# Joining the two halves of each weighted-sum run in a fused LSH attention and mixture-of-experts kernel

## The chip, the core and the metric

The kernel runs on one core of one Trainium2 chip. The metric is the device time of one execution in microseconds (us). Five engines work side by side, each through its own instructions in order: TensorE (PE; its weight loads are listed as PEld), VectorE (DVE), ScalarE (ACT), GpSimd (POOL) and SyncE (SP), which issues most transfers. They meet at semaphores only.

## The reference

```python
# q, k, v: [4, 8, 768, 64]; proj: [64, 6]
q_bucket = bits of (q @ proj > 0);  k_bucket = bits of (k @ proj > 0)
scores = where(q_bucket == k_bucket, q @ k.T / 8, -1e9)
attn = exp(scores - rowmax);  attn /= rowsum + 1e-9
x = attn @ v                      # 3072 tokens of 512
e = argmax(x @ w_gate);  g = softmax(x @ w_gate)[e] * sigmoid(x @ w_output_gate)[e]
out = g * (relu(x @ w1[e]) @ w2[e])      # one expert of 8 for each token
```

## The kernel before, in words

There are 32 heads, taken as 16 pairs. A pair has 12 steps, 192 steps in all; one step is one block of 128 queries of one head against its 768 keys. The order of each engine's work is written out by hand: the program order is the order on each engine.

What one step does, on four engines:

- `scores` (L534): four groups of matmuls (L546) make the 128x768 scores and the bucket penalty in PSUM tile `ps_s` (two buffers). VectorE caps them, copies them to `sc` and takes the row minimum `mn` (L550).
- `soft` (L553): ScalarE takes the exponential of `sc` and its row sum (L558).
- `normal` (L562): for two steps together, VectorE makes the reciprocal of the sums (L565, L566) and GpSimd scales `sc` (L568).
- `transposed` (L570), for the step LAG = 4 earlier: TensorE transposes the six 128x128 blocks of `sc` (L579) into two `ps_t` tiles (two buffers, three blocks each), and ScalarE copies each tile to `pts` (L580).

Six steps are a half pair: 384 queries of both heads. When its `pts` are complete, `weighted` (L582) multiplies them with `v`, chunk by chunk of 128 keys (L590): six chunks, two heads side by side, each head on 64 columns of the array, all added up in `ps_a` (one buffer). `RUN` = 3 puts chunks 0 to 2 at one step and chunks 3 to 5 three steps later. After the last chunk ScalarE copies `ps_a` to `ot` (L593).

The positions in a half pair are counted here from the step that holds chunk 0: position 0 is a step s with (s - 4) divisible by 6, the next ones are positions 1 to 5. The second group of chunks is at position 3.

Side work, hung on step numbers by `plan` (at the end of a step) or `plan_ahead` (before the normalising of a step):

- For the next pair: `project` (L405) on TensorE, 128x32 weights into `ps_m` (one buffer), `threshold` (L415) on VectorE, `split_hi` (L489) on GpSimd, four `split_lo` (L498) on VectorE, and `spread` (L506), transfers on SP that build the operands of the scores.
- `rows` (L595): VectorE transposes `ot` and SP writes it to `x_dram`.
- For each batch of four pairs the routing: `logits` (L618; 128x32 weights, copied to `lt` by ScalarE), `tokens` (L628), `best`, `choose`, `prefix`, `softmax_sum`, `gates`, `ranks`, `cols`, `hot`, `table`, `entries`. Most of it is small VectorE work; `logits`, `tokens`, `prefix` and `table` are TensorE's. `pick` (L769) chooses the first expert after the third batch.

The loop that runs a step (L873 to L895) decides where the exponentials stand: after the transposes of positions 2 and 5 (the steps ahead of a run), and behind the chunks at positions 0 and 3. So there are three exponentials around every group of three chunks.

After the last step the last half pair's chunks, its routing and the first expert's first layer are mixed by hand (L909 to L947): `fill` (L903) is one block of that layer, and the weights `w2` come in through the two `w_raw` buffers. Then eight experts follow.

## Time and profile before

| | |
|---|---|
| median of three runs | 781.82 us (781.23 to 781.83) |
| profiled execution | 783.98 us, of which span 782.2 us |
| TensorE / ScalarE / VectorE / GpSimd busy | 97% / 61% / 58% / 46% of the span |
| mean granted TensorE clock | 0.991 |

The span is the profile's own length of the execution. A busy TensorE is not a TensorE at its peak, since matmuls overlap and their ends are modelled; what a stretch costs is read from the distance between starts of the same instruction.

### The profile page before, as it was taken

What the parts mean: (1) busy time and instruction counts of PE and PEld (TensorE: products, weight loads), DVE (VectorE), ACT (ScalarE), POOL (GpSimd) and SP (SyncE); (2) the same over time, 40 slices, a digit from 0 to 9 for tenths busy, and PEclk for the clock granted to TensorE, in tenths of its full rate; (3) what the DMA queues carried; (4) which work ended last, traced back from release to release, by engine and by line L of the source; (5) the groups of instructions that cost most, each with busy time, mean ns of one, the idle gap of its engine ahead of it and who ended that gap; (6) DMA issues with size and microseconds to landing.
All of it is one profiled execution on the core that took longest, in us unless ns stands there. A gap on an engine that the chain in (4) does not pass through costs nothing. (4 is left out here: it accounts for less than half of the span.)

```text
span 782.2 us, 13687 instructions
## 1 busy us (share of the span) xinstructions
PE 761.1 (97%) x4706; PEld 604.8 (77%) x4706; DVE 451.6 (58%) x1003; ACT 478.9 (61%) x968; POOL 361.9 (46%) x415
## 2 busy tenths in 40 slices
PE   8999999999999999999999989799999999999996
PEld 6677776777766777766777668688999999989894
DVE  6666656666765776766677544146263636455540
ACT  6888888888878888788887731143252524343331
POOL 6564544454443445444455542632537363736301
PEclk9999999999999999999999999899999999999998
DMA  4544555565445556544554232353445444436411
GB/s 164 150 130 90 129 135 97 123 147 139 95 114 132 97 128 146 129 95 116 139 113 123 72 77 109 88 194 114 145 149 157 152 148 153 157 142 208 169 50 40
DMA packets 84799, 98.89 MB, mean 126 GB/s; under 512 B 57999, under 2 KB 59439, under 8 KB 84720
## 3 DMA queue, kind: packets, MB, share of 16 engines
q1 hardware_dynamic: 79376, 84.58, 41.2%
q0 software_dynamic: 5200, 13.31, 5.2%
q8 instruction: 40, 0.66, 0.3%
q14 instruction: 39, 0.32, 0.1%
q10 hardware_dynamic: 144, 0.02, 0.0%
HBM read 59.49 MB, written 13.11 MB: 93 GB/s over the span
## 5 line engine op out<-in xcount | busy, mean ns | idle before, releaser
L568 POOL TENSOR_SCALAR sc<-sc,rsum 128x768 f32<-128x768 f32 x192 | 172.6, 911 | 220.9 <-DVE rsum L566 126.1
L550 DVE TENSOR_SCALAR_CACHE_REDUCE sc<-ps_s 128x768 f32<-128x768 f32 x192 | 183.6, 957 | 124.2 <-PE ps_s L546 117.1
L580 ACT COPY pts<-ps_t 128x384 f32<-128x384 f32 x384 | 165.1, 483 | 67.8 <-PE ps_t L579 67.8
L558 ACT ACTIVATE sc<-sc,mn 128x768 f32<-128x768 f32 x192 | 178.2, 936 | 10.1 <-DVE sc L550 9.8
L579 PEld LDWEIGHTS ps_t<-ident,sc 128*128 128x128 f32 x1152 | 130.4, 140 | 49.3 <-issue 32.2
L579 PE MATMUL ps_t<-ident,sc 128*128 128x128 f32 x1152 | 161.6, 276 | 2.8 <-POOL sc L568 1.9
L590 PE MATMUL ps_a<-pts,vt 128*64 128x384 f32 x768 | 138.0, 494 | 0.4 <-ACT pts L580 0.4
L546 PE MATMUL ps_s<-xr,xl 128*128 128x384 f32 x384 | 114.9, 380 | 1.0 <-DVE sc L550 1.0
L546 PE MATMUL ps_s<-yr,yl 76*128 76x384 f32 x384 | 99.0, 338 | 0.2
L313 PE MATMUL ps_s<-xh,w1h 128*128 128x256 f32 (+7 forms) x288 | 97.2, 337 | 2.0 <-DVE mx L650 1.2
L590 PEld LDWEIGHTS ps_a<-pts,vt 128*64 128x64 f32 x768 | 49.4, 136 | 61.0 <-issue 54.4
L313 PE MATMUL ps_s<-xh,w1l 128*128 128x256 f32 (+7 forms) x288 | 95.2, 331 | 0.8 <-issue 0.8
L324 DVE SCALAR_TENSOR_TENSOR hl<-ps_s,hh 128x256 fp32r<-128x256 f32 (+8 forms) x40 | 34.0, 849 | 107.0 <-ACT hh L323 94.7
L313 PE MATMUL ps_s<-xlo,w1h 128*128 128x256 f32 (+7 forms) x288 | 95.4, 331 | 0.0
L287 POOL DMA_INDIRECT xq<-x_dram,idx x75 | 81.5, 1086 | 21.6 <-issue 20.5
L330 POOL DMA_INDIRECT out_dram<-yo,sid x29 | 32.3, 1113 | 126.9 <-ACT yo L329 65.3
L323 ACT ACTIVATE hh<-ps_s 128x256 fp32r<-128x256 f32 (+8 forms) x40 | 28.9, 725 | 91.1 <-PE ps_s L313 73.2
L546 PEld LDWEIGHTS ps_s<-xr,xl 128*128 128x128 f32 x384 | 58.0, 191 | 16.7 <-DVE sc L550 7.5
L546 PEld LDWEIGHTS ps_s<-yr,yl 76*128 76x128 f32 x384 | 69.9, 189 | 0.7 <-POOL yr L446 0.7
L313 PEld LDWEIGHTS ps_s<-xh,w1h 128*128 128x128 f32 x288 | 54.2, 188 | 4.6 <-issue 2.0
L313 PEld LDWEIGHTS ps_s<-xlo,w1h 128*128 128x128 f32 x288 | 54.1, 188 | 1.3 <-DVE xlo L270 0.2
L313 PEld LDWEIGHTS ps_s<-xh,w1l 128*128 128x128 f32 x288 | 54.1, 188 | 1.2
(204 smaller groups left out, 996.5 us busy)
## 6 DMA issues: line engine op xcount, KB each, us to landing
w_raw<-in_w_dram SPq DMA_DIRECT2D x36, 512.0 KB
qk<-in_qkT_dram SPq DMA_DIRECT2D x32, 384.0 KB
xh<-in_w_dram SPq DMA_DIRECT2D x14, 512.0 KB
xlo<-in_w_dram SPq DMA_DIRECT2D x14, 512.0 KB
vt<-in_v_dram SPq DMA_DIRECT2D x16, 384.0 KB
xr<-xl SPq DMA_DIRECT2D x30, 192.0 KB
yr<-xl SPq DMA_DIRECT2D x30, 192.0 KB
xr<-yl SPq DMA_DIRECT2D x30, 192.0 KB
```

Source lines behind the costliest of these rows:

```text
L287: nc.gpsimd.indirect_dma_start(out=xq[:, k * P:(k + 1) * P], out_offset=None, in_=x_dram.rearrange("n (a f) -> (n a) f", a=NB32), in_offse ...
L313: nc.tensor.matmul(ps, l, r, start=first and k == 0, stop=last and k == len(pairs) - 1)
L323: nc.scalar.activation(hh, ph, AF.Relu)
L324: return lambda: nc.vector.scalar_tensor_tensor(hl, ph, 0.0, f32(hh), ALU.max, ALU.subtract)
L330: nc.gpsimd.indirect_dma_start(out=out[:, :], out_offset=bass.IndirectOffsetOnAxis(ap=sid[0:n, r, a:a + 1], axis=0), in_=yo[0:n], in_offse ...
L546: nc.tensor.matmul(ss[:, n, 0:HS], l[0:k, qs], r[0:k, n * HS:(n + 1) * HS], start=first, stop=not first)
L550: nc.vector.tensor_scalar(sc, ss[:, :, 0:HS], MASKED, None, ALU.min, ALU.min, accum_out=mn)
L558: nc.scalar.activation(pr, pr, AF.Exp, bias=mn, scale=-1.0, accum_out=sums[s // GROUP][:, k:k + 1])
L568: nc.gpsimd.tensor_scalar(live[s0 + k], live[s0 + k], rs[:, k:k + 1], 0.0, ALU.mult, ALU.add)
L579: nc.tensor.transpose(tr[:, c], pr[:, (3 * h + c) * P:(3 * h + c + 1) * P], ident)
L580: nc.scalar.copy(pts[:, 3 * h:3 * h + 3, t * P:(t + 1) * P], tr)
L590: nc.tensor.matmul(st["av"][j * D:(j + 1) * D], st["v"][:, j, c], blocks[hb][j][:, c], start=(c == 0), stop=(c == NT - 1))
```

## The change

The six chunks of a half pair become one run, at position 0. Projections of the next pair, and the second logits of a batch, stand in the run behind the chunks. `threshold` follows behind the run. All four `split_lo` of a pair stand before or in the middle of the VectorE work ahead of the run, and so do `choose`, `ranks`, `cols`, `hot`, `softmax_sum`, `gates`, `entries`. The copies of `ot` and of the logits' `lt` go from ScalarE to VectorE. The exponentials move: one after position 1, one after position 3, three after position 5, one in the run.

```diff
                                      start=True, stop=True)
-                nc.scalar.copy(st["lt"][0:32 * n, cs], pm[0:32 * n])
...
+        def copies():
+            while summed_up:
+                summed_up.pop(0)(nc.vector.tensor_copy)
+
+        for g in range(NP):
+            for hf in range(2 if g + 1 < NP else 1):
+                for c in range(NT):
+                    plan_run(12 * g + 6 * hf + 6 + LAG, lambda hb=2 * g + hf, c=c: weighted(hb, c))
         for g in range(NP):
             s0 = 12 * (g - 1)
             if g >= 2:
                 plan(s0 - 9, lambda g=g: load(g))
-            if g >= 1:
-                hi, lo, sent = ((-1, 2), (4, 4, 4, 7), (4, 7)) if g > 1 else ((2, 4), (4, 5, 6, 7), (5, 7))
-                s0 += g == 1
-                plan(s0 if g > 1 else 3, lambda g=g: project(g))
-                plan(s0 + 1 if g > 1 else 3, lambda g=g: threshold(g))
+                plan_run(s0 + 4, lambda g=g: project(g))
+                plan_behind(s0 + 4, lambda g=g: threshold(g))
                 plan(s0 + 10, lambda g=g: load_v(g))
                 for j in range(2):
-                    plan(s0 + hi[j], lambda g=g, j=j: split_hi(g, j))
+                    plan(s0 + (-1, 2)[j], lambda g=g, j=j: split_hi(g, j))
                     for n in range(2):
-                        (plan_ahead if g > 1 else plan)(s0 + lo[2 * j + n], lambda g=g, j=j, n=n: split_lo(g, j, n))
-                    plan(s0 + sent[j], lambda g=g, j=j: spread(g, j))
-            for hf in range(2 if g + 1 < NP else 1):
-                for c in range(NT):
-                    products.setdefault(12 * g + 6 * hf + 6 + LAG + c // RUN * RUN, []).append(
-                        lambda hb=2 * g + hf, c=c: weighted(hb, c))
-                if g + 1 < NP:
-                    plan(12 * g + 25, lambda g=g, hf=hf: rows(g, hf))
+                        (plan_middle if j else plan_ahead)(s0 + 4, lambda g=g, j=j, n=n: split_lo(g, j, n))
+                    plan(s0 + (4, 5)[j], lambda g=g, j=j: spread(g, j))
+            elif g == 1:
+                plan(3, lambda: project(1))
+                plan(3, lambda: threshold(1))
+                plan(11, lambda: load_v(1))
+                for j in range(2):
+                    plan((3, 5)[j], lambda j=j: split_hi(1, j))
+                    for n in range(2):
+                        plan(5 + 2 * j + n, lambda j=j, n=n: split_lo(1, j, n))
+                    plan((6, 8)[j], lambda j=j: spread(1, j))
+            if g + 1 < NP:
+                for hf in range(2):
...
         for b in range(B - 1):
             r = routing(b)
-            ns = ((2, 4, 8, 9, 10, 13, 19, 25, 22, 22, 34, 34, 35, 35) if b == B - 2 else
-                  (2, 4, 8, 9, 10, 22, 22, 31, 34, 34, 46, 46, 47, 47))
-            for n, fn in zip(ns, (lambda r=r: r["logits"](0, H // 2), lambda r=r: r["tokens"](0, H // 2),
-                                  lambda r=r: r["logits"](1, H // 2), lambda r=r: r["tokens"](1, H // 2),
-                                  r["best"], r["choose"], r["softmax_sum"], r["gates"], r["prefix"], r["ranks"],
-                                  r["cols"], r["hot"], r["table"], r["entries"])):
-                (plan_ahead if n % 3 == 1 and n != 4 else plan)(12 * (H // 2) * (b + 1) + n, fn)
+            s0 = 12 * (H // 2) * (b + 1)
+            soon = b == B - 2
+            plan(s0 + 5, lambda r=r: r["logits"](0, H // 2), copies)
+            plan_run(s0 + 10, lambda r=r: r["logits"](1, H // 2))
+            for hf in range(2):
+                plan(s0 + 7 + 5 * hf, lambda r=r, hf=hf: r["tokens"](hf, H // 2))
+            plan(s0 + 13, r["best"])
+            plan_ahead(s0 + 16, r["choose"])
+            plan(s0 + 17, r["prefix"])
+            plan_middle(s0 + 22, r["softmax_sum"], r["gates"])
+            plan_ahead(s0 + 22, r["ranks"])
+            plan_ahead(s0 + (28 if soon else 34), r["cols"])
+            plan_middle(s0 + (28 if soon else 34), r["hot"])
+            plan(s0 + (30 if soon else 36), r["table"])
+            plan_ahead(s0 + (34 if soon else 40), r["entries"])
 
         r = routing(B - 1)
         s0 = 12 * (NP - 1)
         lp = H // 2 - 1
-        for d, fn in ((4, lambda: r["logits"](0, lp)), (6, lambda: r["tokens"](0, lp)), (8, lambda: r["logits"](1, lp)),
-                      (9, lambda: r["tokens"](1, lp))):
-            plan(s0 + d, fn)
+        for hf in range(2):
+            plan_run(s0 + 4 + 6 * hf, lambda hf=hf: r["logits"](hf, lp))
...
         plan_ahead(late, pick)
-        plan(late + 14, early_gather)
+        plan(late + 15, early_gather)
         for cc in range(NCC):
             plan(late + (1 + cc if cc < 2 else 18), lambda cc=cc: early_load(cc))
-            plan(late + (9, 12, 22, 23)[cc], lambda cc=cc: early_hi(cc))
-            plan_ahead(late + 18 + 6 * (cc // 2), lambda cc=cc: early_lo(cc))
+            plan(late + (9, 10, 22, 23)[cc], lambda cc=cc: early_hi(cc))
+            (plan_middle if cc % 2 else plan_ahead)(late + 18 + 6 * (cc // 2), lambda cc=cc: early_lo(cc))
         for a in range(EARLY):
-            plan(late + 21 + 3 * a, lambda a=a: early_turn(a))
...
-            def softs():
-                while late_soft:
-                    s = late_soft.pop(0)
+            def softs(n):
+                for s in late_soft[:n]:
                     live[s] = soft(s, *live[s])
                     if s % GROUP == GROUP - 1:
                         summed.append(s + 1 - GROUP)
+                del late_soft[:n]
+
+            def normals(n):
+                for s in summed[:n]:
+                    normal(s)
...
-                for fn in ahead.get(s, ()):
-                    fn()
-                while summed:
-                    normal(summed.pop(0))
                 if s in products:
+                    normals(1)
+                    for fn in ahead.get(s, ()):
+                        fn()
+                    normals(GROUP)
+                    for fn in middle.get(s, ()):
+                        fn()
                     for fn in products[s]:
                         fn()
-                    softs()
-                    while summed_up:
-                        summed_up.pop(0)(nc.scalar.copy)
+                    softs(1)
+                    copies()
+                    for fn in behind.get(s, ()):
+                        fn()
+                else:
+                    normals(GROUP)
                 if 0 <= s - LAG < NSTEP:
                     transposed(s - LAG, live.pop(s - LAG))
-                if s < 6 + LAG or s + 1 in products or s >= NSTEP - 1:
-                    softs()
+                since = (s - LAG) % 6
+                if s < 6 + LAG or s >= NSTEP - 1:
+                    softs(GROUP)
+                elif since:
+                    softs((0, 1, 0, 1, 0, 3)[since])
                 for fn in at.get(s, ()):
```

`plan_middle`, `plan_run` and `plan_behind` fill lists like `plan_ahead` does; `products` is the list of a run. `mn` gets 8 buffers instead of 4.

## Rows read from the trace of the kernel before

**Rows 1.** Windows by stage: microseconds from the span's start, and for PE, PEld, DVE, ACT and POOL the busy time with the count of instructions, then the granted TensorE clock as a share, the DMA share and GB/s. The row is the stretch from the first run to the run of step 190.

```profile
27.00:438.00 411.00, 409.76 (x2777) 291.69 (x2777) 275.53 (x745) 336.27 (x766) 194.66 (x246) 1.00 0.51 119
```

**Rows 2.** Timeline of TensorE's matmuls, positions 1 to 4 of a half pair: start, length, engine, line, what, count.

```profile
206.05 0.60 PE L546 MATMUL ps_s<-xr,xl 128*128 128x384 f32 x2
...
206.84 0.82 PE L579 MATMUL ps_t<-ident,sc 128*128 128x128 f32 x6
207.41 0.60 PE L546 MATMUL ps_s<-xr,xl 128*128 128x384 f32 x2
...
208.28 2.16 PE L590 MATMUL ps_a<-pts,vt 128*64 128x384 f32 x12
210.37 0.87 PE L579 MATMUL ps_t<-ident,sc 128*128 128x128 f32 x6
211.00 0.60 PE L546 MATMUL ps_s<-xr,xl 128*128 128x384 f32 x2
...
211.87 0.85 PE L579 MATMUL ps_t<-ident,sc 128*128 128x128 f32 x6
212.47 0.42 PE L546 MATMUL ps_s<-xr,xl 128*128 128x384 f32 x1
```

**Rows 3.** Timeline of TensorE's weight loads in that run of three chunks; a chunk takes two such rows.

```profile
208.66 0.14 PEld L590 LDWEIGHTS ps_a<-pts,vt 128*64 128x64 f32 x2 [0.18 <-issue]
...
209.63 0.14 PEld L590 LDWEIGHTS ps_a<-pts,vt 128*64 128x64 f32 x2 [0.18 <-issue]
```

**Rows 4.** Timeline of TensorE: starts of runs. The first and the last are those of steps 10 and 190, 60 runs apart; the three between follow one another.

```profile
27.09 2.16 PE L590 MATMUL ps_a<-pts,vt 128*64 128x384 f32 x12 [0.41 <-ACT pts L580]
...
67.03 2.16 PE L590 MATMUL ps_a<-pts,vt 128*64 128x384 f32 x12
73.34 2.16 PE L590 MATMUL ps_a<-pts,vt 128*64 128x384 f32 x12
...
438.22 2.16 PE L590 MATMUL ps_a<-pts,vt 128*64 128x384 f32 x12
```

**Rows 5.** Timeline of TensorE: a projection between the transposes and the next scores.

```profile
220.91 0.82 PE L579 MATMUL ps_t<-ident,sc 128*128 128x128 f32 x6
221.66 0.85 PE L411 MATMUL ps_m<-qk,pjc 128*32 128x384 f32 x8
222.44 0.44 PE L546 MATMUL ps_s<-xr,xl 128*128 128x384 f32 x1
```

**Rows 6.** Timeline of ScalarE. The first two rows are of the first steps, where an exponential stands between the copies of two steps; the others are around the run of rows 2.

```profile
20.19 0.96 ACT L558 ACTIVATE sc<-sc,mn 128x768 f32<-128x768 f32 x1
...
21.12 0.87 ACT L580 COPY pts<-ps_t 128x384 f32<-128x384 f32 x2
...
207.37 0.86 ACT L580 COPY pts<-ps_t 128x384 f32<-128x384 f32 x2 [0.50 <-PE ps_t L579]
208.11 0.94 ACT L558 ACTIVATE sc<-sc,mn 128x768 f32<-128x768 f32 x1
...
210.88 0.46 ACT L593 COPY ot<-ps_a 128x384 f32<-128x384 f32 x1
211.24 0.87 ACT L580 COPY pts<-ps_t 128x384 f32<-128x384 f32 x2
```

**Rows 7.** Timeline of TensorE in the first steps: the transposes that waited for the copy of the second of rows 6.

```profile
21.75 0.85 PE L579 MATMUL ps_t<-ident,sc 128*128 128x128 f32 x6
```

**Rows 8.** Timeline of VectorE: the read of the scores of the step whose matmuls start at 207.41.

```profile
208.39 0.96 DVE L550 TENSOR_SCALAR_CACHE_REDUCE sc<-ps_s 128x768 f32<-128x768 f32 x1 [0.39 <-PE ps_s L546]
```

**Rows 9.** Groups of instructions by line, engine and operation: shapes, count, busy us, mean ns of one, idle time before them and what ended it. VectorE's work that moves.

```profile
L503 DVE SCALAR_TENSOR_TENSOR yl<-qk,pj,xl 128x384 fp32r<-128x384 f32 x60 | 38.9, 685 | 0.0
L602 DVE STREAM_TRANSPOSE xb<-ot 128x384 f32<-128x384 f32 x32 | 16.7, 557 | 0.9 <-ACT ot L593 0.7
L418 DVE TENSOR_SCALAR bt<-ps_m,pj 128x384 fp32r<-128x384 f32 x15 | 9.6, 641 | 0.0
L593 DVE COPY ot<-ps_a 128x384 f32<-128x384 f32 x1 | 0.6, 558 | 1.9 <-PE ps_a L590 1.9
```

**Rows 10.** Timeline of VectorE: first instruction of `ranks`, and the sum's instruction behind `ranks` and `pick` (twelve instructions between them); first instruction of `cols`, and the sum's instruction behind `cols` and `hot`.

```profile
382.37 0.20 DVE L696 TENSOR_TENSOR off<-ps_m,base 128x48 f32<-128x48 f32 x1
...
384.62 0.16 DVE L565 TENSOR_SCALAR rsum<-rsum 128x2 f32<-128x2 f32 x1
...
409.01 0.18 DVE L199 TENSOR_TENSOR t_ge<-rank,chki 128x30 f32<-128x30 f32 x1
...
411.42 0.17 DVE L565 TENSOR_SCALAR rsum<-rsum 128x2 f32<-128x2 f32 x1
```

**Rows 11.** Timeline of the end of the steps: TensorE's transposes of step 190 and the first matmul of `fill`; GpSimd's last normalising and the first weights it rounds; ScalarE's cast of the last second-layer weights; TensorE's wait behind it.

```profile
440.31 0.87 PE L579 MATMUL ps_t<-ident,sc 128*128 128x128 f32 x6
449.53 0.36 PE L313 MATMUL ps_s<-xh,w1h 128*128 128x256 f32 x1
445.68 1.79 POOL L568 TENSOR_SCALAR sc<-sc,rsum 128x768 f32<-128x768 f32 x2 [1.19 <-DVE rsum L566]
447.44 1.04 POOL L176 TENSOR_SCALAR w2h<-w_raw 128x1024 fp32r<-128x1024 f32 x1
459.04 1.05 ACT L178 CAST w2h<-w_raw 128x1024 fp32r<-128x1024 f32 x1 [2.48 <-DMA w_raw<-in_w_dram]
460.98 0.36 PE L313 MATMUL ps_s<-xh,w1h 128*128 128x256 f32 x1 [1.19 <-DVE mx L650]
```

## What was predicted before the changed kernel ran

> **What bounds the kernel now.** I read the windows by stage first. From the first run to the run of step 190, TensorE is busy all but 1.2 of 411 us at full granted clock, ScalarE 336, VectorE 276, GpSimd 195 [rows 1]. Since the ends of matmuls are modelled, I then went to TensorE's timeline and took distances between equal starts. A plain step goes from scores to scores in 1.36 us (206.05 to 207.41), and a group of three steps with its run from run to run in 6.31 (67.03 to 73.34) [rows 2, 4]. So a run of three chunks adds 6.31 - 3 x 1.36 = 2.23. Its chunks follow one another at (209.63 - 208.66) / 3 = 0.323, six of them making 1.94 [rows 3]; the other 0.29 is what it costs to enter and leave the run. The 60 strides of the stage sum to 438.22 - 27.09 = 411.1, of which 60 x 6.31 = 378.6; of the rest, 32.5, 22 projections and logits at 0.96 (below) are 21.1; the remaining 11 hold TensorE's work for the logits' transposes, the prefix sums and the tables, one repeated wait of 1.6 (below), and by my estimate 2 to 3 of other waits. So this stage is bound by TensorE, step after step. Each wait that the change adds to TensorE is therefore paid in full, and each switch that it removes is won in full. The experts behind are not touched.
>
> **Part by part.** Below, T1 is the start of the transposes at position 1, T3 and T5 those of positions 3 and 5.
>
> Joined runs. Of two entries and exits in a half pair one goes. It is 31 half pairs in the loop; the last one's second group now stands ahead of the final steps instead of among them, which I count with the end of the steps. 30 x 0.29 = **-8.7 us**. Within a run the work per chunk is the same. If the 0.29 were not a switch but a price per chunk group, it would be 0; I exclude little here, since chunk-to-chunk spacing is constant inside a run and only its edges are long.
>
> Projections and second logits. A projection takes 222.44 - 220.91 = 1.53 from transposes to scores, where a plain step takes 207.41 - 206.84 = 0.57 [rows 2, 5]: 0.96. It is two groups of four 32-column matmuls; at a chunk load's 0.323 each that is 0.65 of work and 0.31 of edges. Behind the chunks it shares the run's exit. What going from 64 columns to 32 columns costs no row shows: nothing at best, one of the two edges (half of 0.29, 0.15) at worst. So each saves 0.16 to 0.31; I take the middle, 0.23, since nothing in the rows favours an end. 14 projections, 3 second logits and both last logits are 19: **-4.4 us** (-3.0 to -5.9).
> The Trainium skill, TensorEngine Tiling (Array Packing), section Tiling Modes, says that changing the tiling mode, and not just the tile, drains the engine. The 0.29 at a run's edges agrees with that; by it the step from 64 to 32 columns drains too, and this term would be -3.0 instead of -4.4.
>
> The copy of `ot` on ScalarE. It starts at 210.88 and pushes the next copies to 211.24; the following step takes 212.47 - 211.00 = 1.47 instead of 1.36 [rows 2, 6]. I count 0.11 once in a pair, 15 times: **-1.6 us** (0 to 31 times, 0 to -3.4). On VectorE the copy costs 0.56 [rows 9].
>
> Exponentials outside the run. This is the part that speaks against the change. Before, all exponentials stand beside a run, in whose 2 us ScalarE has no copies to make. Now one stands behind position 1 and one behind position 3. The copies of a step start 0.53 after its transposes (207.37 - 206.84), the exponential at 1.27 (208.11 - 206.84) [rows 2, 6], and it holds ScalarE for 0.93 (21.12 - 20.19) [rows 6]. So position 2's copies start at T1 + 2.20 instead of 1.36 + 0.53 = 1.89. Position 3's transposes need the tile that the first of these copies frees, and such waiting transposes start 0.63 after the copies (21.75 against 21.12, 211.87 against 211.24) [rows 2, 6, 7]: T1 + 2.83 against a free 2.72, 0.11 late. Transposes that waited take 0.60 to the next scores instead of 0.57 [rows 2], 0.03 more. The same again from T3: 2.83 against 2.75, and 0.03. Sum 0.25 a half pair, 30 times: **+7.5 us**. Bounds: 0, if the copies slip into the slack of the two steps, and 2 x 0.31 = 0.62 a half pair, +18.6, if TensorE lags by the whole delay. The price hardly moves with anything else, as both copies and exponentials have constant lengths. Around the run itself ScalarE gets room: three exponentials from T5 + 1.27 and one more end at T5 + 5.0, and the copies behind the run are due at about T5 + 6.0.
>
> VectorE beside the run. Counted from T5: it reads position 0's scores until 2.6 (the read starts 0.98 after their first matmul and takes 0.96 [rows 2, 8]), makes two sums until 3.0, waits for the third exponential until 4.15, sums until 4.6, and waits for the end of the chunks at 5.6. It then copies `ot` (0.5). In half pairs with `rows` two transposes of 0.56 follow, until 7.1, just when position 1's scores are ready; in those with a projection, four `split_lo` of 0.69 fill the gaps and push the copy, and `threshold` (0.64) ends near 7.2, 0.6 before the scores [rows 9]. So the ordinary side work is hidden. Its cover is 0.6 in one half and nothing in the other; whatever comes late there delays position 1's exponential and with it position 3's transposes, one for one beyond 0.1 of slack (the minimum is ready 0.98 + 0.96 after its first matmul, which is 0.79 ahead of T1, so at T1 + 1.15; the exponential starts at 1.27).
> Routing does come late. Gaps of 1.15 and 1.0 are free. `ranks` with `softmax_sum` and `gates`: `ranks` and `pick` are twelve instructions in 2.25, 0.19 each, so 5 + 8 are 2.4: 0.3 to 0.5 late. `cols` and `hot` take 2.4 [rows 10]: 0.3. For two batches about 1.2 together. The third has `pick` too (3.8 in gaps of 2.15: 1.6) and `cols` and `hot` in the half with `split_lo` (1.3). The two small exponentials of `best` behind position 3, 0.3 each time, the early expert's pieces 0.7: 5.5 us in all. Against it stand the 2.3 of waits in that stage now, which belong to the old placing: **+3.2 us** (-2 to +6).
>
> The end of the steps. Now `fill` starts 449.53 - 440.31 = 9.2 after the transposes of step 190. A run with its wait and the early turn leave this stretch, 2.3. GpSimd's last normalising, which waits for the last scores, exponential and sum, comes only about 1.0 earlier. Behind it come the rounding of `w2`, the freed buffer, its next load, ScalarE's cast (2.48 wait for the transfer), and TensorE's wait of 1.19 [rows 11], which grows by up to 1.3: **+1.2 us** (0 to +1.3).
>
> Transfers. `spread`'s sixteen transfers on SP start after the run's `split_lo` and `threshold`, some 13 us ahead of the first scores that need them; `rows`, `load` and `load_v` queue behind or before as now. I cost them at nothing. If they came late, the next pair's first scores would wait.
>
> Sum: -8.7 - 4.4 - 1.6 + 7.5 + 3.2 + 1.2 = **-2.8 us**. The profiled execution has a span of 782.2 and 783.98 in all, 2.2 over the median of 781.82; the difference is applied to the median: **779.0 us**.
>
> **The rivals.**
> The late copies cost nothing. ScalarE's work of two such steps, two pairs of copies at 0.74 (207.37 to 208.11) and 0.93, is 2.4, under 2.72, and a queue of it might catch up. Against it: the transposes of rows 6 and 7 waited just so. Without that term 781.8 - 10.3 = 771.5.
> New waits take all of the gain. Waits cost 3 more than counted, or the edge from 64 to 32 columns stays and `ot` was rare: about 781.5, no change.
> Slower: VectorE late behind every run. Position 1's minimum sets the exponential, and half the half pairs have no cover. In its present order the copy of `ot` waits for the last matmul of the run and everything behind it waits too. At 0.1 late in each of 30 half pairs the gain is gone; at 0.3, for which `split_lo` and `ot` copies slowed by GpSimd's concurrent scaling would do, it is 30 x 0.2 more than the slack: 779.0 + 6 = 785.0.
> Joining saves nothing: the 0.29 returns inside the longer run. Then 779.0 + 8.7 = 787.7. The constant 0.323 between chunks speaks against it.
>
> **How the numbers follow.** Forecast 0.52, the copies free 0.16, no change 0.17, VectorE late 0.12, joining without gain 0.03. 0.2% is 1.6 us, about what a measurement of this kernel can tell. The forecast's own range, by the edges of its terms, is 776 to 782, and about an eighth of it falls within 1.6 of the present time. Faster: 0.16 + 0.44 = 0.60; same 0.08 + 0.17 = 0.25; slower 0.15. The range reaches from half way to the first rival to most of the slower one: 773 to 784.
>
> **What would show it.** Run starts 12.6 apart in a plain half pair, 12.33 + 0.25 (12.3 if the copies are free); the run's last chunk 11 x 0.323 after its first; a projection following the last chunk within 0.33 (no edge) to 0.45 (an edge); steps of position 2 to 3 and 4 to 5 with 1.47 to 1.50 from scores to scores, others 1.36, and the wait named as `pts`; `ot` on VectorE right behind the run; the wait ahead of `fill`'s later blocks longer than 1.19. It would be wrong if position 1's exponential started later than T1 + 1.3 in plain half pairs, if transposes waited for GpSimd's scaling (it should end 0.2 ahead of need at position 4), or if the scores of a new pair waited for transfers.

## The result: slower by 1.4%

The changed kernel takes 793.04 us (median of four runs, 791.02 to 793.92), the kernel before 781.74 beside it; the ratio is 1.0142, with a 95% interval of 1.0122 to 1.0163. The forecast was 779.0, with a range up to 784. The profiled execution of after took 793.41, of which span 791.7.

From the page of after, busy time of the engines and, in 40 slices, the granted TensorE clock:

```profile
PE 759.4 (96%) x4706; PEld 611.5 (77%) x4706; DVE 504.0 (64%) x1042; ACT 460.0 (58%) x929; POOL 382.9 (48%) x415
...
PEclk9999999999999999999989999999999999999999
```

VectorE is busy 52 us longer than before (451.6). Some 20 of these are the copies that it took over, of which ScalarE shed 19 (478.9 to 460.0). The rest is old work that became slower, and GpSimd too is 21 us longer (361.9 before) with the same 415 instructions. From the page's groups of after, to hold against [rows 9]:

```profile
L576 POOL TENSOR_SCALAR sc<-sc,rsum 128x768 f32<-128x768 f32 x192 | 194.6, 1026 | 213.6 <-DVE rsum L574 149.6
...
L511 DVE SCALAR_TENSOR_TENSOR yl<-qk,pj,xl 128x384 fp32r<-128x384 f32 x60 | 54.8, 952 | 0.3
```

And the scaling in the page of the kernel before:

```profile
L568 POOL TENSOR_SCALAR sc<-sc,rsum 128x768 f32<-128x768 f32 x192 | 172.6, 911 | 220.9 <-DVE rsum L566 126.1
```

`split_lo` (L511, L503 before) went from 685 to 952 ns a piece, GpSimd's scaling (L576, L568 before) from 911 to 1026.

Windows by stage of after (columns as in [rows 1]): the stage from the first run to the run of step 190, and three stretches in it.

```profile
27.00:447.00 420.00, 409.39 (x2770) 299.28 (x2771) 327.23 (x778) 317.01 (x726) 215.10 (x245) 0.98 0.52 117
...
171.00:174.00 3.00, 3.00 (x13) 2.90 (x14) 0.98 (x3) 2.07 (x5) 2.67 (x3) 0.52 1.00 204
...
284.00:287.00 3.00, 3.00 (x14) 2.90 (x14) 1.06 (x3) 2.09 (x5) 2.25 (x3) 0.50 0.88 221
396.00:403.00 7.00, 6.61 (x27) 5.97 (x27) 3.03 (x9) 4.30 (x10) 2.67 (x3) 0.53 0.94 231
```

The stage grew from 411.1 to 420.4 us; from the run of step 190 to the span's end it is 344.2 against 344.0. So the whole loss is in the steps, and in three places there the granted clock is at the lower of its two levels, 1.2 instead of 2.4 GHz. The kernel before has no such stretch in its steps.

Where the 9.2 us are, by the distance from one half pair's run to the next (us; before: its two groups together):

| half pair from the run at step | before | after | what the change put beside VectorE's sums at that run |
|---|---|---|---|
| 22, plain | 13.60 | 12.60 | nothing |
| 28, next to it | 12.73 | 13.43 | `split_lo`; the projection is in the run |
| 70 | 13.60 | 16.21 | `ranks`, `softmax_sum`, `gates` |
| 118 | 13.60 | 16.19 | `ranks`, `softmax_sum`, `gates` |
| 166 | 13.72 | 18.59 | `ranks`, `pick`, `softmax_sum`, `gates` |
| 172 | 12.73 | 16.09 | `cols`, `hot`, `split_lo`; the table follows |
| the other 26 | 357.5 | 353.3 | (22 and 28 among them) |

Before, the projections stood in the half pairs of the first row's kind, after in those of the second's. Two such half pairs together cost 26.03 instead of 26.33. The gain is there, 4.2 us over 26 half pairs; the four half pairs with routing in the run lose 13.4. Some 2.0 us are in both figures: `cols`, `hot`, `entries` and the table's matmuls of the third batch were in the half pair at 178 before, which goes from 14.57 to 12.60, and `cols`, `hot` and the table are now in the one at 172.

### The profile page after: what moved, and what is told of

Same layout as the page of the kernel before. It is cut to its first block, busy times and chain, and to the rows that moved or that the text cites. A ratio compares the mean times of both kernels' runs of the same rounds, so it can differ in the third digit from the quotient of the medians.

```text
span 791.7 us, 13730 instructions
## 1 busy us (share of the span) xinstructions
PE 759.4 (96%) x4706; PEld 611.5 (77%) x4706; DVE 504.0 (64%) x1042; ACT 460.0 (58%) x929; POOL 382.9 (48%) x415
## 5 line engine op out<-in xcount | busy, mean ns | idle before, releaser
L576 POOL TENSOR_SCALAR sc<-sc,rsum 128x768 f32<-128x768 f32 x192 | 194.6, 1026 | 213.6 <-DVE rsum L574 149.6
L587 PE MATMUL ps_t<-ident,sc 128*128 128x128 f32 x1152 | 164.6, 280 | 7.7 <-ACT pts L588 4.9
L587 PEld LDWEIGHTS ps_t<-ident,sc 128*128 128x128 f32 x1152 | 133.5, 143 | 45.5 <-issue 22.3
L598 PE MATMUL ps_a<-pts,vt 128*64 128x384 f32 x768 | 131.1, 490 | 0.4 <-ACT pts L588 0.4
L598 PEld LDWEIGHTS ps_a<-pts,vt 128*64 128x64 f32 x768 | 52.3, 137 | 65.3 <-issue 57.3
L554 PE MATMUL ps_s<-yr,yl 76*128 76x384 f32 x384 | 100.6, 343 | 0.1
L329 POOL DMA_INDIRECT out_dram<-yo,sid x29 | 30.7, 1057 | 125.3 <-ACT yo L328 82.8
L511 DVE SCALAR_TENSOR_TENSOR yl<-qk,pj,xl 128x384 fp32r<-128x384 f32 x60 | 54.8, 952 | 0.3
```

The source lines that it names most:

```text
L329: nc.gpsimd.indirect_dma_start(out=out[:, :], out_offset=bass.IndirectOffsetOnAxis(ap=sid[0:n, r, a:a + 1], axis=0), in_=yo[0:n], in_offse ...
L511: nc.vector.scalar_tensor_tensor(st["yl"][j][:, cs], st["qk"][j][:, cs], sgn, f32(st["xl"][j][:, cs]), ALU.mult, ALU.subtract)
L554: nc.tensor.matmul(ss[:, n, 0:HS], l[0:k, qs], r[0:k, n * HS:(n + 1) * HS], start=first, stop=not first)
L576: nc.gpsimd.tensor_scalar(live[s0 + k], live[s0 + k], rs[:, k:k + 1], 0.0, ALU.mult, ALU.add)
L587: nc.tensor.transpose(tr[:, c], pr[:, (3 * h + c) * P:(3 * h + c + 1) * P], ident)
L598: nc.tensor.matmul(st["av"][j * D:(j + 1) * D], st["v"][:, j, c], blocks[hb][j][:, c], start=(c == 0), stop=(c == NT - 1))
```

## Inside one slow half pair

Timeline of VectorE in after; the run of step 70 stands at 160.57 to 164.6. Columns: start, length, engine, line, what, count.

```profile
162.75 0.40 DVE L709 TENSOR_TENSOR base<-base,tot 128x8 f32<-128x8 f32 x1
163.29 0.76 DVE L573 TENSOR_SCALAR rsum<-rsum 128x2 f32<-128x2 f32 x1
...
164.59 0.19 DVE L681 RECIPROCAL den<-den 128x6 f32<-128x6 f32 x1
164.69 0.70 DVE L684 TENSOR_TENSOR en<-en,oneh 128x48 f32<-128x48 f32 x1
165.43 0.20 DVE L686 TENSOR_REDUCE es<-en 128x6 f32<-128x48 f32 x1
165.67 0.58 DVE L687 TENSOR_SCALAR es<-es 128x6 f32<-128x6 f32 x1
...
166.51 0.61 DVE L689 TENSOR_TENSOR gate<-den,es 128x6 f32<-128x6 f32 x1
167.04 0.55 DVE L601 COPY ot<-ps_a 128x384 f32<-128x384 f32 x1
...
168.46 0.91 DVE L558 TENSOR_SCALAR_CACHE_REDUCE sc<-ps_s 128x768 f32<-128x768 f32 x1
```

Timeline of GpSimd in the same stretch:

```profile
162.21 1.81 POOL L576 TENSOR_SCALAR sc<-sc,rsum 128x768 f32<-128x768 f32 x2 [3.94 <-DVE off L704]
164.44 1.79 POOL L576 TENSOR_SCALAR sc<-sc,rsum 128x768 f32<-128x768 f32 x2 [0.42 <-DVE den L679]
166.20 0.91 POOL L503 TENSOR_SCALAR xl<-qk,pj 128x768 fp32r<-128x768 f32 x1
```

Operations on 2 to 48 numbers a partition take 0.4 to 0.76 us while GpSimd works on 768 (two pairs of scalings, then `split_hi`, L503). They are not slowed by a factor: they end when an instruction of GpSimd ends. L573 ends at 164.05 and the scaling beside it at 164.02, L687 at 166.25 against 166.23, L689 at 167.12 against 167.11. Not all operations are held up: the reduction L686 and the reciprocal L681 stand in the same scaling and take 0.20 and 0.19. So the copy of `ot` begins 2.4 us after the run's end, and position 1's scores are read at 168.46. Timeline of TensorE behind it:

```profile
167.37 0.82 PE L587 MATMUL ps_t<-ident,sc 128*128 128x128 f32 x6
169.44 0.62 PE L554 MATMUL ps_s<-xr,xl 128*128 128x384 f32 x2 [1.25 <-DVE sc L558]
...
170.96 1.40 PE L587 MATMUL ps_t<-ident,sc 128*128 128x128 f32 x6 [0.54 <-ACT pts L588]
172.01 0.99 PE L554 MATMUL ps_s<-xr,xl 128*128 128x384 f32 x2
```

The scores of position 3 wait for a free `ps_s` (1.25 us), its transposes for `pts` (0.54), and then the same matmuls take 1.40 instead of 0.82 and 0.99 instead of 0.60: the clock has fallen. One lateness is paid twice.

## The experiments

The theory (A) from these rows: VectorE's routing work at the run is what is late, since GpSimd's scaling, which now runs beside it, holds it up. Against it stood that there is simply too much work at that place, and that the loss is in the longer run or the moved exponentials. Plain half pairs of the changed kernel and of the one with the routing elsewhere all take 12.59 to 12.61, so distances between runs of chunks can be compared from one experiment to the next, also where there is one run only.

**The routing's VectorE work out of the runs.** The pieces go to the ends of other steps, the rest of the change stays.

```diff
-            plan_ahead(s0 + 16, r["choose"])
+            plan(s0 + 15, r["choose"])
...
-            plan_middle(s0 + 22, r["softmax_sum"], r["gates"])
-            plan_ahead(s0 + 22, r["ranks"])
-            plan_ahead(s0 + (28 if soon else 34), r["cols"])
-            plan_middle(s0 + (28 if soon else 34), r["hot"])
-            plan(s0 + (30 if soon else 36), r["table"])
-            plan_ahead(s0 + (34 if soon else 40), r["entries"])
+            plan(s0 + 20, r["ranks"])
+            plan(s0 + 26, r["softmax_sum"])
+            plan(s0 + 27, r["gates"])
+            plan(s0 + 32, r["cols"])
+            plan(s0 + 33, r["hot"])
+            plan(s0 + 35, r["table"])
+            plan(s0 + (36 if soon else 39), r["entries"])
...
-        plan_ahead(late, pick)
+        plan(late - 1, pick)
```

> The changed kernel with the routing's VectorE work (choose, ranks, pick, softmax_sum, gates, cols, hot, entries) taken from the runs and put behind the transposes of positions 3 to 5, where GpSimd scales nothing; everything else as changed. Theory A (this work, stretched by GpSimd's scaling beside it, makes VectorE late behind four runs and TensorE wait, and the wait halves its clock): the strides of the runs of steps 70, 118 and 166 fall from 16.2, 16.2 and 18.6 to 12.6 to 12.9 us, that of step 172 from 16.1 to 14.8, no stretch at half clock, and the whole takes 776 to 780 us, below the kernel before. Theory B (a run of 4 us starves what follows it, whatever stands beside it): strides stay above 14 and the time above 787.

Measured: 778.13 us against 782.82, ratio 0.9941 (0.9924 to 0.9959). The four half pairs take 12.62, 12.61, 12.62 and 13.89, together 51.7 instead of 67.1; the stage is 404.7, 6.4 less than before, and no stretch of it is at the lower clock. Five more half pairs, whose runs had `choose` (64, 112, 160) or `entries` (88, 136) beside them, gain 3.1 together; three that now take `cols` and `hot` (76, 124) or the table (178) lose 2.9. Timeline of VectorE, the same `ranks` instruction now ahead of position 0, one sum, and the copy:

```profile
158.68 0.17 DVE L709 TENSOR_TENSOR base<-base,tot 128x8 f32<-128x8 f32 x1
...
162.34 0.73 DVE L573 TENSOR_SCALAR rsum<-rsum 128x2 f32<-128x2 f32 x1 [1.27 <-ACT sc L566]
...
163.76 0.56 DVE L601 COPY ot<-ps_a 128x384 f32<-128x384 f32 x1 [0.49 <-PE ps_a L598]
```

L709 takes 0.17 where GpSimd is idle. The sum that still stands beside a scaling takes 0.73, but it is over by 163.07 and VectorE then waits 0.49 for the run's end. So the longer run and the moved exponentials are not the loss: with the routing elsewhere the change is faster than the kernel before.

**GpSimd's scaling left out** ahead of the runs at steps 70, 118, 166 and 172 (the output's weights of those steps stay unscaled), with the routing in the runs.

```diff
-        def normal(s0):
+        def normal(s0, scaled=True):
...
-            for k in range(GROUP):
+            for k in range(GROUP if scaled else 0):
...
-                for s in summed[:n]:
-                    normal(s)
+                for g in summed[:n]:
+                    normal(g, s not in (70, 118, 166, 172))
```

> The changed kernel, which leaves out GpSimd's scaling (not the sums) at the runs of steps 70, 118, 166 and 172, so that the routing's VectorE work stands beside an idle GpSimd; order and amount of VectorE's work are as changed. Theory A: instructions with two inputs from SBUF and the short copies and scalar forms, 0.4 to 0.76 us there now, fall to about 0.2; the stride of step 70 falls from 16.2 to 12.8 to 13.3, that of step 166 from 18.6 to 13.5 to 14.5, without a stretch at half clock, 10 us or more off the whole. Rival (it is the amount of work in the gap, not GpSimd): durations change little and the strides stay above 15.

Measured: 781.48 in one run, span 779.8; the four half pairs take 12.69, 12.68, 13.54 and 14.59. Timeline of VectorE, the same instructions as above (this run begins 0.20 earlier):

```profile
163.09 0.17 DVE L573 TENSOR_SCALAR rsum<-rsum 128x2 f32<-128x2 f32 x1 [0.37 <-ACT sc L566]
...
163.91 0.17 DVE L684 TENSOR_TENSOR en<-en,oneh 128x48 f32<-128x48 f32 x1
...
164.34 0.17 DVE L687 TENSOR_SCALAR es<-es 128x6 f32<-128x6 f32 x1
...
164.77 0.17 DVE L689 TENSOR_TENSOR gate<-den,es 128x6 f32<-128x6 f32 x1
164.86 0.55 DVE L601 COPY ot<-ps_a 128x384 f32<-128x384 f32 x1
```

The same work in the same place, with GpSimd idle beside it: every one is back at 0.17, the copy comes 2.0 earlier against its run. It is not how much work there is but what runs beside it. The Trainium skill, SBUF — State Buffer, section Who interferes with whom, says that a VectorE instruction with two inputs in SBUF, and copies, casts and scalar operations in their fast modes, share a port pair with GpSimd, that whoever comes first holds it for its whole instruction, and that reductions never contend on trn2. The trace agrees as far as it goes: L684 and L689, with two inputs there, and L573 and L687, scalar operations, each last until GpSimd's instruction is over, and the reduction L686 does not. Which mode an operation ran in no view shows. The expectations below call this the port theory.

**The waits filled.** Fourteen transposes of the identity at the ends of steps 72, 120 and 168, where TensorE would wait; all else as in after.

```diff
+                if s in (72, 120, 168):
+                    warm = ps_m.tile([P, 3, P], F32, name="ps_m")
+                    for i in range(14):
+                        nc.tensor.transpose(warm[:, i % 3], ident, ident)
```

> The changed kernel with fourteen transposes of the identity (1.5 us of TensorE work into an unused buffer) at the end of steps 72, 120 and 168, into the wait behind the late VectorE. If the half clock behind the wait is a good part of the loss: no stretch at half clock behind steps 70 and 118, their strides 14.2 to 15 instead of 16.2, that of step 166 16.5 to 17.5 instead of 18.6, 3 to 6 us off the whole although work is added. Rival (the clock costs little, the waits are all): strides stay or grow by 0.5 to 1.5.

Measured: 789.94 in one run, span 788.1 against 791.7 of after; the half pairs at 70, 118 and 166 take 14.73, 14.73 and 15.93 instead of 16.21, 16.19 and 18.59. Timeline of TensorE, and the window of the stretch that was at the lower clock:

```profile
167.86 1.69 PE L939 MATMUL ps_m<-ident 128*128 128x128 f32 x14
169.31 0.60 PE L554 MATMUL ps_s<-xr,xl 128*128 128x384 f32 x2
169.74 0.52 PE L554 MATMUL ps_s<-yr,yl 76*128 76x384 f32 x2
170.80 0.84 PE L587 MATMUL ps_t<-ident,sc 128*128 128x128 f32 x6 [0.54 <-ACT pts L588]
```

```profile
171.00:174.00 3.00, 3.00 (x23) 2.72 (x22) 1.71 (x5) 2.57 (x7) 2.54 (x3) 1.00 1.02 246
```

The scores start where they would have, the wait for `pts` is still 0.54, and the clock stays at 1.00: ten more matmuls fit in the same 3 us than in after. This splits the loss. For the four half pairs together, after is 67.1, with the waits filled 61.5, with no scaling beside 53.5, with the routing elsewhere 51.7. So 5.6 us are the clock, all of them at 70, 118 and 166 (172 stays at 16.08), 8.0 the lateness that the scaling makes, and 1.8 the routing's own time, the table at 172 included.

**One exponential outside the run, not two.** This sizes the term of +7.5 by itself.

```diff
-                    softs((0, 1, 0, 1, 0, 3)[since])
+                    softs((0, 1, 0, 0, 0, 4)[since])
```

> The changed kernel with the exponential behind position 3 moved to the group behind position 5, so that one instead of two stands outside the run. If each exponential outside costs TensorE 0.12 by the late copies: plain half pairs fall from 12.60 to 12.48 us, steps 4 to 5 to 1.36, 3 to 4 us off the whole. Rival (the group around the run is full, so that the copies behind it come late): plain half pairs stay at 12.6 or grow.

Measured: 802.53 in one run, span 800.8 against 791.7 of after. A plain half pair goes from 12.60 to 12.47, 0.13 for an expected 0.12. But the whole is slower, not 3 to 4 us faster: one with `split_lo` goes from 13.43 to 14.03. Timelines of GpSimd, VectorE and TensorE in one of those, whose run ends at 43.58 with the projection behind it:

```profile
41.91 4.81 POOL L576 TENSOR_SCALAR sc<-sc,rsum 128x768 f32<-128x768 f32 x4 [3.63 <-DVE rsum L574]
...
43.62 2.33 DVE L511 SCALAR_TENSOR_TENSOR yl<-qk,pj,xl 128x384 fp32r<-128x384 f32 x2
45.86 0.55 DVE L601 COPY ot<-ps_a 128x384 f32<-128x384 f32 x1
...
49.50 0.85 PE L587 MATMUL ps_t<-ident,sc 128*128 128x128 f32 x6 [0.61 <-ACT pts L588]
```

With the sums later, the second pair of `split_lo` falls wholly into four scalings on end: 1.17 us each, and the scalings 1.20. So `split_lo` has the same trouble as the routing. The copy of `ot` comes 2.28 behind the run's end; in after it is 1.44 (71.29 against 69.85), which the projection just covers.

**The projection at the end of position 3,** as long as it is not in the run (with the routing elsewhere).

```diff
-                plan_run(s0 + 4, lambda g=g: project(g))
-                plan_behind(s0 + 4, lambda g=g: threshold(g))
+                plan(s0 + 1, lambda g=g: project(g), lambda g=g: threshold(g))
```

> The kernel with the routing taken from the runs (776.5 us of span), with the projections and their thresholds put back outside the runs, at position 3 (entries at step 36 of each batch so that the one PSUM buffer is free). This prices the projection behind the chunks, where it adds 13.43 - 12.60 = 0.83 us: outside it should add 0.96 to 0.98, so that half pairs with one take 13.57 instead of 13.43, and 14 of them 2 us more in all. Rival (VectorE's threshold and the late position cost more than the edge): half pairs with a projection take 13.8 or more.

Measured: 781.63 in one run, span 779.9 against 776.5. The plain half pair, which now has the projection, goes from 12.61 to 13.44, the one with `split_lo` from 13.43 to 12.97: 26.41 instead of 26.04 for both. The run's place is worth 0.37 a pair. But outside the run the projection adds 0.83 to its half pair, as it does inside, and not the 0.96 to 0.98 expected. TensorE's starts show why. Around the transposes of position 3 and the projection behind them, it is 2.45 from scores to scores (60.66 to 63.11), 0.95 more than the 1.50 without the projection (60.41 to 61.91). The next two distances are 1.39 and 1.36, and not 1.36 and 1.50: behind a projection, the exponential of position 3 no longer makes the transposes of position 5 late. So the 0.37 isn't the saved edge. It is the half pair with `split_lo` alone, which is 0.36 over a plain one: there the copy of `ot` comes 1.56 behind the run's end (45.90 against 44.34), and the projection in the run had been hiding that.

**The copies of `ot` and of the second logits back on ScalarE** (with the routing elsewhere).

```diff
-        def copies():
+        def copies(copy=nc.vector.tensor_copy):
             while summed_up:
-                summed_up.pop(0)(nc.vector.tensor_copy)
+                summed_up.pop(0)(copy)
...
-                    copies()
+                    copies(nc.scalar.copy)
```

> The kernel with the routing taken from the runs (776.5 us of span), with the copies of ot and of the second logits back on ScalarE behind the exponential in the run. By the working, ScalarE has about 1 us free there: plain half pairs stay at 12.6, those with a projection at 13.43 or slightly less, the span within 1 us of 776.5. Rival (the copies behind the run come late, as in the kernel before): 0.1 more in each half pair, 3 us.

Measured: 777.07 in one run, span 775.4 against 776.5. A plain half pair is unchanged (12.61), one with `split_lo` 0.05 shorter, and those at 76, 124 and 172 about 0.5 shorter; the stage is 403.1 instead of 404.7. With one exponential in the run and none behind it, the copy costs ScalarE nothing.

**VectorE's side work ahead of both sums,** in the changed kernel with its routing in the runs: GpSimd would then be idle beside it. (It is the first of the two edits that the next kernel adds, and the expectation calls it so.)

```diff
-                    normals(1)
-                    for fn in ahead.get(s, ()):
-                        fn()
-                    normals(GROUP)
-                    for fn in middle.get(s, ()):
+                    for fn in ahead.get(s, []) + middle.get(s, []):
                         fn()
+                    normals(1 + GROUP)
```

> The changed kernel with that first edit alone: routing left in the runs, the same instructions at the same run, but all of VectorE's side work before both sums. GpSimd scales only after it. Port theory: the routing's instructions take about 0.2 us each again, the stride of step 70 falls from 16.2 to 13.2 to 13.8 (scaling that starts late keeps the first transposes 0.5 to 1 us), no stretch at half clock there, 6 to 11 us off 791.7. Rival (the amount of work before the copy of ot decides): strides of 15 and more.

Measured: 791.7 in one run, span 789.9 against 791.7 of after; the gain expected isn't there. The half pairs at 70, 118 and 166 come down to 13.60, 13.60 and 14.93, which is 8.9 less. But the one at 172 rises to 18.49, two others by 1.0 each, and the stride behind step 190 from 16.32 to 18.52. From its groups, and its timelines of GpSimd and TensorE behind the run of step 172:

```profile
L511 DVE SCALAR_TENSOR_TENSOR yl<-qk,pj,xl 128x384 fp32r<-128x384 f32 x60 | 34.9, 632 | 0.0
```

```profile
402.42 3.56 POOL L576 TENSOR_SCALAR sc<-sc,rsum 128x768 f32<-128x768 f32 x4 [7.56 <-DVE rsum L573]
...
403.39 0.87 PE L587 MATMUL ps_t<-ident,sc 128*128 128x128 f32 x6 [2.22 <-POOL sc L576]
```

`split_lo` is at 632 ns and four scalings take 3.56, 0.89 each: no more contention. But with `split_lo`, `cols` and `hot` all ahead of the sums, the scaling starts only at 402.42, and the transposes wait 2.22 for it. Then the granted clock falls too, to 0.50 in 405:407, and again behind step 190, where the wait for the scaling is 3.05. The order that keeps VectorE fast makes GpSimd late when there is too much of it.

**All three together:** routing elsewhere, side work first, one exponential outside.

> The kernel with the routing taken from the runs, and two more edits: VectorE's side work at a run stands before both sums instead of between and behind them, so that it runs while GpSimd has nothing to scale; and one exponential instead of two stands outside the run (the other goes to the group behind position 5). With the port theory: the four split_lo of a projection's half pair take about 0.55 us each instead of 0.9, and the later exponentials no longer push them; half pairs take 12.46 and 13.29 instead of 12.60 and 13.43, 4 us in all: 773 to 775 us, ratio 0.990. Rival (scaling that comes late keeps the transposes behind the run waiting): half pairs with a projection 13.6 or more, the whole above 778.

Measured: 779.23 against 784.18, ratio 0.9942 (0.9927 to 0.9957); no better than the routing alone. The stage is 401.2, 3.5 better, and `split_lo` half pairs are at 13.25; but the stride behind step 190 is 19.50 instead of 16.39. Two splits of the early expert's weights stand ahead of the sums there, TensorE waits 3.68 for the scaling, and the granted clock is 0.50 from 436 to 442. Timelines of VectorE and TensorE:

```profile
433.23 2.36 DVE L872 TENSOR_TENSOR w1l<-w_raw,w1h 128x1024 fp32r<-128x1024 f32 x2
...
437.03 1.33 PE L587 MATMUL ps_t<-ident,sc 128*128 128x128 f32 x5 [3.68 <-POOL sc L576]
```

**The sums first again at step 190 alone,** and then, in a second kernel, the copies on ScalarE too.

```diff
-                    for fn in ahead.get(s, []) + middle.get(s, []):
+                    if s >= NSTEP - 2:
+                        normals(1)
+                    for fn in ahead.get(s, []):
+                        fn()
+                    if s >= NSTEP - 2:
+                        normals(GROUP)
+                    for fn in middle.get(s, []):
                         fn()
```

> The kernel after with the routing's VectorE work at ends of steps, VectorE's side work before the sums, and one exponential outside the run, as in the run with the side work first; but at step 190, the last run in the loop, the sums go first again. That run lost 3.1 us between the run at step 190 and the last one (19.50 against 16.39): two splits of 1.18 us of the early expert's weights stood ahead of two sums, the scaling was late, and TensorE waited 3.7 us for it. If that order is the whole loss there, the last stride comes back to 16.4 and the span to 776.5 - 3.1 = 773.4, about 0.989 of the kernel before. If the wait comes from the exponentials kept for the run, the stride stays above 18 and the time near 779.

> As the run before, and the copies behind the run stay on ScalarE. By the earlier run that did this alone they cost nothing there and save 0.5 us in the loop and 0.7 at its end: span 772 to 773. If four exponentials around the run leave ScalarE no room for them, the plain half pair rises above 12.47 and the time is over that of the run before.

Measured: 776.72 and 777.49, against 783.21; ratios 0.9923 (0.9910 to 0.9937) and 0.9923 (0.9909 to 0.9936). Neither is as fast as expected: the spans of the profiled executions are 774.5 and 776.4, for 773.4 and 772 to 773. In the first, the stride behind step 190 comes back to 17.36, not to 16.4. Part of what stayed is this window, at the lower clock after a wait of 2.2 for the scaling:

```profile
437.00:440.00 3.00, 2.98 (x13) 2.12 (x12) 2.48 (x6) 1.50 (x4) 2.29 (x3) 0.50 0.75 246
```

The copy's place makes no difference here (plain half pairs 12.47 in both, the stage 401.2 and 401.4). Both beat the kernel before by 0.8% and, going by the two ratios, the changed one by 2.2%.

## Why the prediction was wrong, point by point

The step that failed is **VectorE beside the run**: for the four half pairs it counted 0.4, 0.4, 1.6 and 1.3 us, 3.7 of its 5.5, and after pays 15.3 more there than the same kernel with the routing elsewhere (15.7 over the whole stage). (The items given for the 5.5 add up to nearer 5.7. And of the 2.3 of waits that were set against them, the trace of before names 1.1 in that stage, three waits for the scaling; no row shows the rest.) Of the stage's miss of 13.2 (forecast -4.0, measured +9.2) this is all but 1.6. The term failed in two ways:

- Its durations, 0.19 an instruction, came from [rows 10], where `ranks` and `pick` stand ahead of the sum. GpSimd's scaling follows the sum, so it was idle in those rows. The timeline of GpSimd in the kernel before shows it: 3.28 us idle up to the scaling that follows that sum.

```profile
385.18 1.79 POOL L568 TENSOR_SCALAR sc<-sc,rsum 128x768 f32<-128x768 f32 x2 [3.28 <-PE ps_s L546]
```

  The change puts them behind the first sum, beside the scaling. The count of the work was right: without the scaling the four cost 1.8 over the kernel with the routing elsewhere. The 8.0 of lateness were missing.
- A late step was priced at its lateness, one for one. It costs the clock too: 5.6 more.

The path was nearly the one that the prediction had drawn. It had the lateness reach TensorE by position 1's exponential and position 3's transposes, and in step 70's half pair that exponential does start 3.41 behind T1 (169.42 against 166.01; in a plain one 1.30). But the first and longer wait comes before that, at the scores of position 3, for the `ps_s` that VectorE has not read yet.

The slower rival named the slowing of `split_lo` and of `ot` copies beside GpSimd's scaling, and put it in every half pair, with a chance of 0.12. The mechanism was this one. Its place was not: `split_lo` did slow, but the projection hid it, and the copy, which reads `ps_a` in PSUM, kept its 0.55; the routing, where nothing hid it, was not in that rival.

What came out as forecast, or near it:

- **Joined runs.** The plain half pair is 12.60 for a forecast of 12.58. With the exponential's price from the experiment, 12.47 - 0.13 is 12.34, against 12.62 for two groups with their runs before: 0.28 is gone, the forecast's exit and entry (0.29).
- **Exponentials outside.** In after, the distance from scores to scores around the transposes of positions 3 and 5 is 1.50 and 1.49, elsewhere 1.36 (60.60 to 62.10 below is the first), as forecast. One moved back saved 0.13.
- **Projections.** TensorE's timeline of after, two half pairs, shows 0.78 from the projection to the transposes, behind a run of the same 4.02:

```profile
53.23 4.09 PE L598 MATMUL ps_a<-pts,vt 128*64 128x384 f32 x24
57.25 0.87 PE L587 MATMUL ps_t<-ident,sc 128*128 128x128 f32 x6
...
60.60 0.60 PE L554 MATMUL ps_s<-xr,xl 128*128 128x384 f32 x2
...
62.10 0.59 PE L554 MATMUL ps_s<-xr,xl 128*128 128x384 f32 x2
...
65.83 4.09 PE L598 MATMUL ps_a<-pts,vt 128*64 128x384 f32 x24
69.85 0.85 PE L419 MATMUL ps_m<-qk,pjc 128*32 128x384 f32 x8
70.63 0.87 PE L587 MATMUL ps_t<-ident,sc 128*128 128x128 f32 x6
```

  The 0.78 is 0.13 over the 0.65 of its loads, and 0.18 under the 0.96 of [rows 2, 5]; and from the run's start to what follows it is 4.02 whether 128 columns follow or 32. So an edge from 64 to 32 columns is there, near the bound of 0.15, and the term is -3.4 for nineteen rather than -4.4, by this one place. The drain that the Trainium skill states in TensorEngine Tiling (Array Packing), section Tiling Modes, would have been the better guess (-3.0).
- **The copy of `ot`** was priced at -1.6 for leaving ScalarE; in the new order its leaving gains nothing (put back, with the routing elsewhere, the stage is 1.6 shorter), and VectorE, which took it, is the engine that is late.
- **The end of the steps** was forecast at +1.2; from the run of step 190 to the span's end it is +0.2. **Transfers** made nothing late: from the first run to the run of step 190 in after, the waits of TensorE's matmuls name VectorE and ScalarE alone.

## What to carry to other kernels

A duration read from a trace holds for what ran beside it there: before work is moved on VectorE, look at what GpSimd does in the new place, and price two-input and scalar operations there with a wait of up to the length of GpSimd's instruction. The count of the work said 4 us; its neighbour, and the clock behind the waits, made it 15. And where TensorE is the bound, waits like the 1.25 and 0.54 here are to be priced with the slow matmuls behind them. Filling them won back 5.6 us in this kernel, moving the small work to the ends of other steps 15.7.

## What the runs showed of the hardware

- Beside a scaling of 128x768, VectorE operations with two inputs in SBUF, and scalar operations, on as few as two numbers a partition took 0.40 to 0.76 us, and 0.17 without: three of them end within 0.03 us of GpSimd's instruction beside them. Small reductions and reciprocals stay at 0.17 to 0.20, and the copy of `ot` from PSUM at 0.55. The scaling pays too beside `split_lo`: 1.20 against 0.89.
- After a wait of TensorE of 1.25 us and one of 0.54, the granted clock was 0.52 in the 3 us that followed (the lower of the two levels); with the first of them filled by transposes it stayed at 1.00.
